# Eight and 32-row matmuls of a mixture-of-experts tail, issued over 128 rows with zeros behind

## The chip, the cores and the metric

The kernel runs on one core of a Trainium2 chip. The metric is the device time of one execution in microseconds. The engines are TensorE (PE, with its weight loads shown apart as PEld), VectorE (DVE), ScalarE (ACT), GpSimd (POOL) and SyncE (SP); transfers run on 16 DMA engines and are issued from SP or POOL.

## The reference

Three layers follow each other: a linear attention with random features, a dense layer with `h - tanh(h)`, and a mixture of eight experts. The change is in the third:

```python
def _moe2_ref(x, w_gate, w1, w2):
    N, D = x.shape                 # 2304, 512
    E = w_gate.shape[1]            # 8
    cap = N // E                   # 288
    flat = (x @ w_gate).flatten()
    order = np.argsort(-flat)
    assigned = -np.ones(N, dtype=np.int64)
    counts = np.zeros(E, dtype=np.int64)
    for idx in order:              # best score first
        tok, e = (int(idx) // E, int(idx) % E)
        if assigned[tok] >= 0 or counts[e] >= cap:
            continue
        assigned[tok] = e
        counts[e] += 1
    for e in range(E):
        mask = assigned == e
        h = np.maximum(x[mask] @ w1[e], 0.0)
        out[mask] = h @ w2[e]
```

So tokens go to experts by falling score, an expert is full at 288 tokens, and every expert computes two products over its 288 tokens.

## The kernel before

The kernel is one program whose order is set by a planner: every operation is entered with its engine, an assumed duration, the tiles it reads and writes and a due time (`plan.at`), and a list scheduler then writes the instructions of each engine in one fixed order. At run time each engine works through its list and waits on semaphores where a tile isn't ready.

The attention and the dense layer take the first 550 us or so. The dense layer's second product (L648, tiles `acc`) goes on beyond that for the last two of six blocks, until about 630 us. From about 545 us on the routing runs beside it, and from about 636 us the experts.

**Routing (`search_ops`, `route_ops`).** Experts are filled one after another; which one is next, and the score at which it is full, is searched digit by digit, seven digits for each of the first seven experts (the last takes what is left). For each digit DVE compares the scores with 15 to 31 thresholds (L1030), PE counts by nine products into 40 rows (L1036), DVE turns the counts into one number for each of the eight experts, in `d8` (8 rows, one column, L1057), and PE spreads these eight numbers over all 128 rows with one product over 8 rows (L1061: `d8` broadcast as the stationary operand, the 8x8 identity `id8` as the moving one). DVE reads the largest digit out of it (L1064) and makes the next thresholds. That is 7 x 7 = 49 products of 8 rows.

**Places (`place_ops`).** When an expert's tokens are known, 18 products (L1193) put the tokens' numbers in order; a copy (L1198) brings the result of 32 rows into `r1`, and one product over 32 rows (L1200) spreads it over 128. There are 8 of these.

**Gathers and experts (`expert_ops`).** For each expert POOL gathers its 288 rows of 512 numbers from DRAM in three pieces of 128, 128 and 32 rows (`xg`, L1289). PE transposes them: for each of four column groups c one PSUM tile takes three transposes, 128, 128 and 32 tokens wide (L1301 for experts 1 to 7, L1305 for expert 0). The 32-row piece is the third. ACT and DVE copy the 288 columns out as `xgH` and `xgL`. Then come the expert's products, each with 288 columns (L1333 to L1335 and L1352 to L1354), and at the end transposes back (L1364) and a scatter to DRAM. The routing of the following experts and the transposes of the next one are put between these products on PE's list, one small product at a time.

`pairs_ops` clears two tiles `pairs` on POOL (L1003) before the first search; DVE fills them (L993) and PE's counts read them.

The pieces come from a ring of three slots in the order of g, so the 32-row piece has had one slot of its own.

Of the kernel before, what the change touches and what calls it, by code (L numbers as in the profile page):

```python
# [8 lines left out]
F32 = mybir.dt.float32  # L9
F32R = mybir.dt.float32r  # L10
BF16 = mybir.dt.bfloat16
# [174 lines left out]
def tile_kernel(ctx, tc, q, k, v, omega, w_in, w_out, w_gate, w_gate_t, w1, w2, out, dbg=None):  # L186
    nc = tc.nc
# [4 lines left out]
    P = 128  # L192
# [701 lines left out]
    def r_setup():  # L894
# [10 lines left out]
        for i, wd in enumerate(WIDTH):  # L905
# [48 lines left out]
        nc.vector.memset(t["asg"], 0.0)  # L954
        t["mfull"] = c.tile([1, 1], BF16, name="mfull")
        nc.vector.memset(t["mfull"], -1.0e6)
        t["id8"] = c.tile([E, E], BF16, name="id8")
        nc.vector.tensor_copy(t["id8"], ident[:E, :E])
        rt.update(t)

    rings = {}


    SLOTS = {"wraw": (3, 4), "ewH": (0, 4), "ewL": (1, 11), "xg": (NG, NG), "xgH": (1, 2), "xgL": (1, 2),
             "hH": (0, 9), "hL": (0, 9), "yT": (0, 4)}

    def tmp(shape, dt, name, n=1):
        if name not in rings:
            rings[name] = plan.ring(shape, dt, name, [
                (wr[0], [f"r_{name}{i}" for i in range(SLOTS.get(name, (n, n))[0])], False)])  # L970
        return Buf(rings[name])
# [25 lines left out]
    pairs = []  # L997

    def pairs_ops():
        for i in range(2):  # L1000
            t = wr[0].tile([P, NTT, 32], BF16, name=f"pairs{i}")
            pairs.append(Buf(None, t))
            plan.op(POOL, 0.5, lambda e, t=t: nc.gpsimd.memset(t, 0.0), w=[pairs[i]])  # L1003
        first["i288"] = Buf(None, wr[0].tile([P, 1, CAP], I32, name="i288"))
        plan.op(POOL, 0.5, lambda e: nc.gpsimd.iota(first["i288"].t, pattern=[[1, CAP]], base=0, channel_multiplier=0),
                w=[first["i288"]])

    def search_ops(m, A2, rr8):
# [3 lines left out]
        for i, (tab, n, sh) in enumerate(rt["bits"]):  # L1012
# [33 lines left out]
            if 0 < i < len(WIDTH) - 1:  # L1046
# [3 lines left out]
                vec(0.2, lambda V, base=base, tab2=tab2, n2=n2, pre=pre: V.tensor_scalar(  # L1050
                    base.t[:, :n2], tab2, pre.t, flip.t, op0=OP.bitwise_or, op1=OP.bitwise_xor), r=[pre, flip], w=[base], after=cmps)

            cond, d8 = tmp([E, 32], F32, "cond"), tmp([E, 1], BF16, "d8")
            odd = tmp([E, 32], F32, "odd")
            vec(0.1, lambda V, odd=odd, cnt=cnt, n=n: V.tensor_scalar(
                odd.t[:, :n], cnt.t[32:32 + E, n:2 * n], -1.0, None, op0=OP.mult), r=[cnt], w=[odd])
            vec(0.16, lambda V, cond=cond, cnt=cnt, d8=d8, n=n, odd=odd: V.scalar_tensor_tensor(  # L1057
                cond.t[:, :n], cnt.t[:E, :n], rt["r8"], odd.t[:, :n], op0=OP.subtract, op1=OP.is_ge,
                accum_out=d8.t), r=[cnt, odd, rr8], w=[cond, d8])
            dig = Buf(rpr)  # L1060
            plan.op(PE, 0.05, lambda e, dig=dig, d8=d8: nc.tensor.matmul(  # L1061
                dig.t[:, :E], d8.t.to_broadcast([E, P]), rt["id8"], start=True, stop=True), r=[d8], w=[dig])
            d = tmp([P, 1], I32, "d", 3)
            vec(0.08, lambda V, d=d, dig=dig: V.tensor_reduce(d.t, dig.t[:, :E], axis=AX.X, op=OP.max), r=[dig], w=[d])  # L1064
            if i == 0:
# [104 lines left out]
    def place_ops(p, inc, acc):  # L1170
# [20 lines left out]
        def rows(e):  # L1191
            for j in range(NTT):
# [1 line left out]
                                 start=(j == 0), stop=(j == NTT - 1))  # L1194

        plan.op(PE, 0.55, rows, r=[lid, ohh], w=[pi])
        r1 = tmp([2 * LO, NHI], BF16, "r1")
        vec(0.08, lambda V: V.tensor_copy(r1.t, pi.t[:2 * LO, :NHI]), r=[pi], w=[r1])  # L1198

        plan.op(PE, 0.15, lambda e: nc.tensor.matmul(pr.t[:, :NHI], rt["spread"][:2 * LO], r1.t, start=True, stop=True),  # L1200
                r=[r1], w=[pr])
        rs = rt["rsel"]
        vec(0.08, lambda V: V.tensor_tensor(rs[:, :NHI], pr.t[:, :NHI], rt["hm"], op=OP.mult), r=[pr], w=[brsel])
# [77 lines left out]
    def expert_ops(p):  # L1281
# [2 lines left out]
        xg = []  # L1284
        plan.at = base + AT_GET if p else -98.0
        for g in range(NG):
            t = tmp([GS, DM], F32, "xg", NG)
            ix = idxs[p][g][1] if p else first["top"][g]
            plan.op(POOL, 1.03, lambda e, g=g, t=t, ix=ix: nc.gpsimd.indirect_dma_start(  # L1289
                out=t.t[:GN[g]], out_offset=None, in_=ms if p else ms[:(NTT - TPB) * P + 1, :],  # L1290
                in_offset=bass.IndirectOffsetOnAxis(ap=ix.t[:GN[g]].bitcast(U32), axis=0)),
                r=[ix], w=[t], after=stored if p else stored4, late=5.0)
            xg.append(t)
        plan.at = base + AT_TURN if p else -58.0
        for c in range(NC):
            tp = Buf(bank3)
            cs = slice(c * P, (c + 1) * P)

            def transposes(e, c=c, tp=tp):
                for g in range(NG):  # L1300
                    nc.tensor.transpose(tp.t[:, g * GS:g * GS + GN[g]], xg[g].t[:GN[g], c * P:(c + 1) * P], ident[:GN[g], :GN[g]])  # L1301

            def others(e, cs=cs, tp=tp):
                for g in range(NG):
                    nc.tensor.matmul(tp.t[:, g * GS:g * GS + GN[g]], xg[g].t[:GN[g], cs], ident[:GN[g], :GN[g]],  # L1305
                                     start=(g == 0), stop=False, is_transpose=True, skip_group_check=True)

            def lasts(e, cs=cs, tp=tp, t=0, i=0):
                nc.tensor.matmul(tp.t[:, :CAP], m5[t][i].t[:, cs], first["sel"].t[:, t, :], start=False,
                                 stop=(t == TPB - 1 and i == 1), skip_group_check=True)  # L1310

            if p:
                plan.op(PE, 0.38, transposes, r=xg, w=[tp])
            else:
                o = plan.op(PE, 0.38, others, r=xg, w=[tp])
                for t in range(TPB):
                    for i in range(2):
                        o = plan.op(PE, 0.12, lambda e, lasts=lasts, t=t, i=i: lasts(e, t=t, i=i),
                                    r=[m5[t][i], first["sel"]], w=[tp], after=[o])
            plan.op(ACT, 0.3, lambda e, c=c, tp=tp: copy(e, xH.t[:, c], tp.t[:, :CAP]), r=[tp], w=[xH])  # L1320
            plan.op(DVE, 0.37, lambda e, c=c, tp=tp: low(e, xL.t[:, c], tp.t[:, :CAP], xH.t[:, c]), r=[tp, xH], w=[xL])
# [274 lines left out]
```

## Time and profile before

| | |
|---|---|
| runs | 921.21 us median of 3 (918.92 to 921.49) |
| profiled execution | 916.65 us, its span 914.7 us |
| busy share of the span | PE 96%, PEld 84%, DVE 71%, ACT 51%, POOL 28% |
| granted TensorE clock, mean | 0.986 of full speed |
| transfers | 194.72 MB, mean 213 GB/s |

The page's slices show PE at 0.9 or more of nearly every slice, with one at 0.5 where the first search begins. Ends of matmuls in the trace are modelled and overlap the next start, so a matmul's price in a dense stream is read from the distance of two starts, and not from its duration.

### The profile page before, as it was taken

How to read it: one execution, taken by the hardware profiler on the slowest of the kernel's cores; microseconds unless marked ns; L12 is line 12 of the kernel's file. 1: busy time of each engine (PE TensorE's matmuls, PEld its weight loads, DVE VectorE, ACT ScalarE, POOL GpSimd, SP SyncE). 2: the span in 40 equal slices, each digit the busy share in tenths (PEclk: the TensorE clock that was granted, in tenths of full speed). 3: DMA queues.
4: the chain of work that ended last, by engine and by line, in shares of the span. 5: the costliest groups of instructions: out<-in, count | busy, mean ns of one | idle time of the engine just before them, and what ended most of it. 6: DMA issues, size and time to landing. Idle time of an engine off the chain costs nothing. (4 is left out here: it accounts for less than half of the span.)

```text
span 914.7 us, 17555 instructions
## 1 busy us (share of the span) xinstructions
PE 875.9 (96%) x6168; PEld 770.8 (84%) x6168; DVE 652.2 (71%) x1931; ACT 469.3 (51%) x1015; POOL 253.2 (28%) x271
## 2 busy tenths in 40 slices
PE   8988999999999999999999959899999999999995
PEld 6887888988989888989989937676889888999995
DVE  6899999866588779777778763527687786784520
ACT  5876554545457445655577640203366554465521
POOL 1223433333431345244313230000122322321211
PEclk9999999999999999999999999999999999999998
DMA  8988777876375666434677745845788886877600
GB/s 256 344 283 285 255 248 258 264 246 199 109 241 162 209 207 219 150 105 127 209 289 269 266 164 170 272 127 174 236 266 233 270 226 186 279 186 262 213 28 26
DMA packets 104365, 194.72 MB, mean 213 GB/s; under 512 B 28370, under 2 KB 42834, under 8 KB 104275
## 3 DMA queue, kind: packets, MB, share of 16 engines
q1 hardware_dynamic: 98610, 174.71, 58.0%
q0 software_dynamic: 5664, 18.88, 8.6%
q8 instruction: 49, 0.80, 0.4%
q14 instruction: 42, 0.34, 0.1%
HBM read 150.03 MB, written 34.08 MB: 201 GB/s over the span
## 5 line engine op out<-in xcount | busy, mean ns | idle before, releaser
L648 PE MATMUL acc<-wo,gL 128*128 128x512 f32 x288 | 114.9, 401 | 0.2 <-POOL gL L303 0.2
L601 PE MATMUL bk<-xH,wi 128*128 128x384 f32 x320 | 113.9, 356 | 0.9 <-DVE xt L500 0.9
L602 PE MATMUL bk<-xL,wi 128*128 128x384 f32 x320 | 107.8, 337 | 0.0
L603 PE MATMUL bk<-xH,iL 128*128 128x384 f32 x320 | 107.7, 337 | 0.0
L707 DVE SCALAR_TENSOR_TENSOR lw<-wf,raw 128x512 f32<-128x512 f32 x128 | 103.5, 808 | 2.9 <-POOL wf L704 1.4
L648 PE MATMUL acc<-wo,gH 128*128 128x512 f32 x240 | 101.1, 421 | 0.0
L303 POOL TENSOR_TENSOR gL<-s,gH 128x384 fp32r<-128x384 f32 x52 | 62.7, 1206 | 137.1 <-ACT gH L298 136.0
L648 PE MATMUL acc<-oL,gH 128*128 128x512 f32 x240 | 95.9, 400 | 0.3 <-DVE oL L303 0.3
L438 ACT ACTIVATE phi<-bk,nm 128x128 f32<-128x128 f32 x272 | 77.2, 384 | 34.4 <-DVE nm L441 34.1
L704 POOL TENSOR_TENSOR wf<-oL,wo 128x512 f32<-128x512 f32 x48 | 66.1, 1378 | 68.0 <-DMA oL<-low_wo 63.7
L298 ACT ACTIVATE gH<-s 128x384 fp32r<-128x384 f32 x80 | 42.2, 527 | 63.7 <-DVE s L628 46.3
L626 DVE SCALAR_TENSOR_TENSOR s<-s,bk 128x384 f32<-128x384 f32 x80 | 44.0, 550 | 41.7 <-ACT s L625 40.8
L648 PEld LDWEIGHTS acc<-wo,gL 128*128 128x128 f32 x288 | 54.9, 191 | 13.6 <-POOL gL L303 0.7
L601 PEld LDWEIGHTS bk<-xH,wi 128*128 128x128 f32 x320 | 60.7, 190 | 6.1 <-PE bk L480 1.1
L602 PEld LDWEIGHTS bk<-xL,wi 128*128 128x128 f32 x320 | 60.7, 190 | 2.7
L605 ACT ACTIVATE u<-bk 128x384 f32<-128x384 f32 x80 | 39.2, 491 | 45.2 <-PE bk L603 43.0
L603 PEld LDWEIGHTS bk<-xH,iL 128*128 128x128 f32 x320 | 60.4, 189 | 0.0
L628 DVE SCALAR_TENSOR_TENSOR s<-s,u 128x384 f32<-128x384 f32 x80 | 57.8, 722 | 1.1
L441 DVE TENSOR_REDUCE nm<-bk 128x4 f32<-128x512 f32 (+1 forms) x75 | 46.4, 631 | 12.7 <-PE bk L427 11.1
L648 PEld LDWEIGHTS acc<-wo,gH 128*128 128x128 f32 x240 | 45.7, 190 | 7.0
L648 PEld LDWEIGHTS acc<-oL,gH 128*128 128x128 f32 x240 | 46.0, 191 | 6.4 <-DVE oL L303 0.6
L625 ACT ACTIVATE s<-u,qbias 128x384 f32<-128x384 f32 x80 | 49.3, 616 | 3.8 <-DVE gL L303 1.4
(355 smaller groups left out, 2345.5 us busy)
## 6 DMA issues: line engine op xcount, KB each, us to landing
r_wraw<-in_moe_w_dram SPq DMA_DIRECT2D x48, 512.0 KB, 6.3
iL<-low_wi SPq DMA_DIRECT2D x80, 256.0 KB, 3.2
oL<-low_wo SPq DMA_DIRECT2D x80, 256.0 KB, 2.7
raw<-in_moe_w_in_dram SPq DMA_DIRECT2D x32, 512.0 KB, 5.1
raw<-in_moe_w_out_dram SPq DMA_DIRECT2D x32, 512.0 KB, 4.3
dw<-in_moe_w_dram SPq DMA_DIRECT2D x16, 512.0 KB, 5.9
w1l<-dw SPq DMA_DIRECT2D x16, 512.0 KB, 3.0
s_wraw<-in_moe_w_dram SPq DMA_DIRECT2D x16, 512.0 KB, 5.7
```

Source lines behind the costliest of these rows:

```text
L303: (nc.gpsimd if e == POOL else nc.vector).tensor_tensor(out, in_, high.bitcast(F32), op=OP.subtract)
L438: nc.scalar.activation(ph.t[:, i0 + i, :], pj.t[:, i * M:(i + 1) * M], AF.Exp, bias=nmx.t[:, i0 + i:i0 + i + 1])
L441: plan.op(DVE, 0.1 + 0.125 * n, lambda e, pj=pj, i0=i0, n=n: V.tensor_reduce(nmx.t[:, i0:i0 + n], pj.t[:, :n * M].rearrange("p (i m) -> p ...
L601: nc.tensor.matmul(ph(), piece(iH, c), xH.t[:, c, :], start=(c == 0), stop=False)
L602: nc.tensor.matmul(ph(), piece(iH, c), xL.t[:, c, :], start=False, stop=False)
L603: nc.tensor.matmul(ph(), piece(iL, c), xH.t[:, c, :], start=False, stop=(c == NC - 1))
L625: plan.op(ACT, 0.52, lambda e: nc.scalar.activation(s.t, ut(), AF.Square, bias=qbias), r=[u], w=[s], lag=2.8)
L626: plan.op(DVE, 0.52, lambda e: V.scalar_tensor_tensor(s.t, s.t, QD, ph(), op0=OP.add, op1=OP.mult), r=[p, s], w=[s], lag=3.4)
L628: plan.op(DVE, 0.65, lambda e: V.scalar_tensor_tensor(s.t, s.t, QC, ut(), op0=OP.mult, op1=OP.mult), r=[u, s], w=[s], lag=4.0)
L648: nc.tensor.matmul(acc[t].t, (gL if k == 2 else gH).t[:, c], (oL if k == 1 else oH).t, start=(f == 0 and k == 0), stop=(f == NF - 1 and k ...
L704: plan.op(POOL, 1.45, lambda e: nc.gpsimd.tensor_tensor(w.t, lo.t.bitcast(F32), wo[:, f, :].bitcast(F32), op=OP.add), r=[lo, wbuf["wo", f] ...
L707: x_reads.append(plan.op(DVE, 0.9, lambda e, i=i: nc.vector.scalar_tensor_tensor(scratch.t.bitcast(F32), w.t, 1.0, half(rows[i // 2], i % ...
```

## The change

Three kinds of small products are issued over 128 rows:

- `d8`, before a ring tile of 8 rows, is one lasting tile of 128 rows that is cleared once; DVE writes its first 8 rows as before. `id8` holds the first 8 columns of the 128x128 identity. L1061's product then has 128 rows.
- `r1` is one lasting tile of 128 rows, cleared once, of which the copy writes the first 32; L1200's product reads all 128 rows of it and of `spread`.
- The third piece of a gather is one lasting tile of 128 rows (`xg_rest`), cleared once on POOL in `pairs_ops`; the gather writes its first 32 rows. The three transposes of a column group all read 128 rows and write 128 columns of the PSUM tile; the copies still read 288 columns.

```diff
-        t["id8"] = c.tile([E, E], BF16, name="id8")
-        nc.vector.tensor_copy(t["id8"], ident[:E, :E])
+        t["id8"] = c.tile([P, E], BF16, name="id8")
+        nc.vector.tensor_copy(t["id8"], ident[:, :E])
+        for name, n in (("d8", 1), ("r1", NHI)):
+            t[name] = Buf(None, c.tile([P, n], BF16, name=name))
+            nc.vector.memset(t[name].t, 0.0)
...
-    SLOTS = {"wraw": (3, 4), "ewH": (0, 4), "ewL": (1, 11), "xg": (NG, NG), "xgH": (1, 2), "xgL": (1, 2),
+    SLOTS = {"wraw": (3, 4), "ewH": (0, 4), "ewL": (1, 11), "xg": (NG - 1, NG - 1), "xgH": (1, 2), "xgL": (1, 2),
...
     def pairs_ops():
+        first["xg"] = Buf(None, wr[0].tile([P, DM], F32, name="xg_rest"))
+        plan.op(POOL, 0.6, lambda e: nc.gpsimd.memset(first["xg"].t, 0.0), w=[first["xg"]])
...
-            cond, d8 = tmp([E, 32], F32, "cond"), tmp([E, 1], BF16, "d8")
+            cond, d8 = tmp([E, 32], F32, "cond"), rt["d8"]
...
-                accum_out=d8.t), r=[cnt, odd, rr8], w=[cond, d8])
+                accum_out=d8.t[:E]), r=[cnt, odd, rr8], w=[cond, d8])
...
-                dig.t[:, :E], d8.t.to_broadcast([E, P]), rt["id8"], start=True, stop=True), r=[d8], w=[dig])
+                dig.t[:, :E], d8.t.to_broadcast([P, P]), rt["id8"], start=True, stop=True), r=[d8], w=[dig])
...
-        plan.op(PE, 0.15, lambda e: nc.tensor.matmul(pr.t[:, :NHI], rt["spread"][:2 * LO], r1.t, start=True, stop=True),
+        plan.op(PE, 0.15, lambda e: nc.tensor.matmul(pr.t[:, :NHI], rt["spread"], r1.t, start=True, stop=True),
...
-            t = tmp([GS, DM], F32, "xg", NG)
+            t = tmp([GS, DM], F32, "xg", NG - 1) if g < NG - 1 else first["xg"]
...
-                    nc.tensor.transpose(tp.t[:, g * GS:g * GS + GN[g]], xg[g].t[:GN[g], c * P:(c + 1) * P], ident[:GN[g], :GN[g]])
+                    nc.tensor.matmul(tp.t[:, g * GS:(g + 1) * GS], xg[g].t[:, c * P:(c + 1) * P], ident,
+                                     start=True, stop=True, is_transpose=True)
```

The order of the instructions stays as it was on PE, ACT and SP. On POOL, at the place where the second half of the program begins, the list before is:

```order
L1003 MEMSET pairs_11785 128x576
L1003 MEMSET pairs_11786 128x576
L1005 IOTA i_11787 128x288
L1289 DMA r_xg_12390<-ms,r_ix_12290 128x512
L1289 DMA r_xg_12397<-ms,r_ix_12293 128x512
L1289 DMA r_xg_12410<-ms,r_ix_12295 32x512
```

and now:

```order
L1004 MEMSET xg_rest 128x512
L1008 MEMSET pairs_11790 128x576
L1008 MEMSET pairs_11791 128x576
L1010 IOTA i_11792 128x288
L1294 DMA r_xg_12386<-ms,r_ix_12288 128x512
L1294 DMA r_xg_12393<-ms,r_ix_12291 128x512
L1294 DMA xg_rest<-ms,r_ix_12293 32x512
```

One clearing stands ahead of the two of `pairs`; the third gather has a new target and the same place. On PE, in the transposes of one expert (tiles `bd` are PSUM banks), the list before is:

```order
L1301 MATMUL bd_16541<-ident,r_xg_16434 128x128
L1301 MATMUL bd_16541<-ident,r_xg_16446 128x128
L1301 MATMUL bd_16541<-ident,r_xg_16455 128x32
L1301 MATMUL bd_16547<-ident,r_xg_16434 128x128
L1301 MATMUL bd_16547<-ident,r_xg_16446 128x128
L1301 MATMUL bd_16547<-ident,r_xg_16455 128x32
```

and now:

```order
L1306 MATMUL bd_16484<-ident,r_xg_16378 128x128
L1306 MATMUL bd_16484<-ident,r_xg_16390 128x128
L1306 MATMUL bd_16484<-ident,xg_rest 128x128
L1306 MATMUL bd_16490<-ident,r_xg_16378 128x128
L1306 MATMUL bd_16490<-ident,r_xg_16390 128x128
L1306 MATMUL bd_16490<-ident,xg_rest 128x128
```

Nothing moved there; every third transpose writes 128 columns where it wrote 32.

## Rows read from the trace of the kernel before

**Rows 1.** Stretch, length; PE, PEld, DVE, ACT, POOL busy (instructions); clock, DMA share, GB/s.

```profile
554.00:583.00 29.00, 29.00 (x167) 20.79 (x167) 13.54 (x74) 1.52 (x3) 0.00 (x0) 1.00 0.60 184
...
636.00:690.00 54.00, 53.60 (x463) 47.37 (x460) 41.73 (x192) 28.19 (x44) 13.90 (x17) 1.00 0.84 245
```

**Rows 2.** PE's waits, 540 to 645, then 640 to 905: total us, times, longest.

```profile
PE rp L1036 <- DVE pairs L993: 6.4, 2, 4.4
PE rp L1061 <- DVE r_cond L1057: 1.5, 3, 0.6
...
PE be L1364 <- ACT s_yT L298: 0.2, 1, 0.2
```

**Rows 3.** Lines L1061 (with its waiter), L1200, L1301, L1305: ns min/median/max, starts, forms.

```profile
L1061 PE MATMUL rp<-id,r_d x49: 161/175/183, 548.3 to 810.9; 8*128 8x8 bf16 x49
...
  DVE r_d L1064: 37.8, 41
...
L1200 PE MATMUL rp<-r_r,spread x8: 178/178/179, 584.0 to 857.1; 32*128 32x18 bf16 x8
...
L1301 PE MATMUL bd<-ident,r_xg x45: 243/271/329, 664.2 to 867.2; 128*128 128x128 f32 x30, 32*128 32x32 f32 x15
...
L1301 PE MATMUL be<-ident,r_xg x39: 243/273/329, 664.7 to 868.8; 128*128 128x128 f32 x26, 32*128 32x32 f32 x13
...
L1305 PE MATMUL bd<-ident,r_xg x12: 243/272/328, 601.5 to 633.5; 128*128 128x128 f32 x8, 32*128 32x32 f32 x4
```

**Rows 4.** PE in order of time around one digit product: start us, us, what.

```profile
645.92 0.29 PE L1335 MATMUL be<-r_xgH,s_ewL 128*128 128x288 f32 x1
646.15 0.17 PE L1061 MATMUL rp<-id,r_d 8*128 8x8 bf16 x1
646.25 0.40 PE L1333 MATMUL be<-r_xgH,wi 128*128 128x288 f32 x1
646.49 0.30 PE L1334 MATMUL be<-r_xgL,wi 128*128 128x288 f32 x1
```

**Rows 5.** PE in order of time around the full-row pair L1125, L1126.

```profile
778.22 0.29 PE L1354 MATMUL bd<-s_hH,s_ewL 128*128 128x288 f32 x1
778.35 0.19 PE L1125 MATMUL rp<-r_M,onesb 128*128 128x36 bf16 x1
778.39 0.18 PE L1126 MATMUL rp<-r_M,tri 128*128 128x36 bf16 x1
778.42 0.38 PE L1352 MATMUL bd<-s_hH,wi 128*128 128x288 f32 x1
778.63 0.29 PE L1353 MATMUL bd<-s_hL,wi 128*128 128x288 f32 x1
```

**Rows 6.** PE in order of time, the twelve gather transposes of expert 6.

```profile
838.03 1.64 PE L1301 MATMUL bd<-ident,r_xg 128*128 128x128 f32 x9
839.60 0.61 PE L1301 MATMUL be<-ident,r_xg 128*128 128x128 f32 x3
840.14 0.40 PE L1352 MATMUL be<-s_hH,s_ewH 128*128 128x288 f32 x1
840.38 0.29 PE L1353 MATMUL be<-s_hL,s_ewH 128*128 128x288 f32 x1
```

**Rows 7.** PE in order of time, twelve transposes of results, all of 128 rows.

```profile
847.01 1.03 PE L1364 MATMUL bd<-ident,s_yT 128*128 128x128 f32 x8
847.88 0.60 PE L1364 MATMUL be<-ident,s_yT 128*32 128x128 f32 x4
848.24 0.38 PE L1333 MATMUL bd<-r_xgH,wi 128*128 128x288 f32 x1
848.45 0.30 PE L1334 MATMUL bd<-r_xgL,wi 128*128 128x288 f32 x1
```

**Rows 8.** POOL and DVE in order of time where the first search begins.

```profile
543.75 1.09 POOL L1003 MEMSET pairs<- 128x576 bf16 x2 [2.94 <-SPq L1459]
...
546.72 0.31 DVE L993 TENSOR_TENSOR pairs<-r_a,r_am 128x144 bf16<-128x144 f32 x1
```

More of the change, by code (lines that the diff above doesn't have):

```diff
@@ L1196, in place_ops @@
         plan.op(PE, 0.55, rows, r=[lid, ohh], w=[pi])
-        r1 = tmp([2 * LO, NHI], BF16, "r1")
-        vec(0.08, lambda V: V.tensor_copy(r1.t, pi.t[:2 * LO, :NHI]), r=[pi], w=[r1])
-        plan.op(PE, 0.15, lambda e: nc.tensor.matmul(pr.t[:, :NHI], rt["spread"][:2 * LO], r1.t, start=True, stop=True),
+        r1 = rt["r1"]
+        vec(0.08, lambda V: V.tensor_copy(r1.t[:2 * LO], pi.t[:2 * LO, :NHI]), r=[pi], w=[r1])
+        plan.op(PE, 0.15, lambda e: nc.tensor.matmul(pr.t[:, :NHI], rt["spread"], r1.t, start=True, stop=True),
                 r=[r1], w=[pr])
@@ L1300, in transposes @@
                 for g in range(NG):
-                    nc.tensor.transpose(tp.t[:, g * GS:g * GS + GN[g]], xg[g].t[:GN[g], c * P:(c + 1) * P], ident[:GN[g], :GN[g]])
+                    nc.tensor.matmul(tp.t[:, g * GS:(g + 1) * GS], xg[g].t[:, c * P:(c + 1) * P], ident,
+                                     start=True, stop=True, is_transpose=True)
             def others(e, cs=cs, tp=tp):
                 for g in range(NG):
-                    nc.tensor.matmul(tp.t[:, g * GS:g * GS + GN[g]], xg[g].t[:GN[g], cs], ident[:GN[g], :GN[g]],
+                    nc.tensor.matmul(tp.t[:, g * GS:(g + 1) * GS], xg[g].t[:, cs], ident,
                                      start=(g == 0), stop=False, is_transpose=True, skip_group_check=True)
```

## Prediction

> **What bounds the kernel now.** I read the table by stretch first. From 554 us to the end of the last expert TensorE (PE) has work in nearly every microsecond: 29.0 of 29.0 us while the last two blocks of the dense layer finish, 53.6 of 54.0 us in the first experts [rows 1]. A busy PE need not be a PE that gets on, so I read the waits next. From 640 to 905 us PE waits for another engine once, for 0.2 us; from 540 to 645 us the waits that matter are 6.4 us for VectorE's tile `pairs`, in two places where a search starts, and three short ones before the digit product L1061 [rows 2]. So from about 554 us on the time is what PE's own queue takes, in its fixed order, and every nanosecond between the starts of two neighbouring matmuls counts. The third view is therefore PE's instructions in order of time, read by the distances of their starts; busy times would hide what is looked for.
>
> There the small products show a cost that their size doesn't explain. In the stream of an expert's products the starts lie 0.13 us apart. Around one digit product (8 rows, 8 columns) they read 645.92, 646.15 for the product, 646.25 and 646.49: from the product before to the second one after, 0.57 us instead of 0.26, so one tiny product costs 0.31 us [rows 4]. A pair of equally small bf16 products that use all 128 rows (L1125 and L1126, 36 columns) reads 778.22, 778.35, 778.39, 778.42, 778.63: 0.41 us over the same stretch with two of them inside, and the first starts after the usual 0.13 us, not after 0.23 [rows 5]. The transposes say the same. Twelve of them with a 32-row piece in every third place take from 838.03 to 840.14, 2.11 us; twelve with 128 rows throughout take from 847.01 to 848.24, 1.23 us [rows 6, 7]. So the queue stops when it goes from 128 rows to fewer, and again on the way back.
>
> **The change part by part.** No instruction changes its place on PE, ACT, DVE or SP; the product of 8 or 32 rows is issued in the same place with 128. What is added is one clearing of the 128x512 piece on POOL, two small clearings and a wider copy of the 8x8 identity on DVE in the setup.
>
> *Digit products (L1061).* There are 49 [rows 3]. Three start a search and are waited for by PE anyway [rows 2]; these keep their wait, and gain at most what the way back costs, about 0.1 us, 0.3 us in all. Of the other 46, 39 stand alone in a stream of full products and 7 beside another small product. For one that stands alone the stretch goes from 0.57 us [rows 4] to that of one full-row product. The trace has that with two products inside, 0.41 us, and leaving out the 0.03 to 0.04 us of one gives 0.37 to 0.38 [rows 5]. The gain is thus 0.16 us at least (nothing saved for the one product fewer) and 0.20 at most; I take 0.19, which is 39 x 0.19 = 7.4 us. The 7 beside another product I count half, 0.7 us. Sum: 8.4 us.
>
> *The index product (L1200).* There are 8, each of 32 rows and 18 columns [rows 3]. Seven stand in the experts' stream at the price of a digit product: 7 x 0.19 = 1.3 us. The first is followed by a chain on DVE that PE waits for; I give it 0.1 us. Sum: 1.4 us.
>
> *The 32-row transposes (L1301, L1305).* There are 15 + 13 = 28 of them for experts 1 to 7 and 4 for expert 0 [rows 3], one behind each pair of full ones. Over twelve transposes and to the second product behind them the time is 840.38 - 838.03 = 2.35 us now, and 848.45 - 847.01 = 1.44 us where all have 128 rows [rows 6, 7]: 0.91 us for each of seven experts, 6.4 us. That already holds the price of moving 128 columns in place of 32. For expert 0 three of the four stand in the dense layer's stream, 3 x 0.23 = 0.7 us; the fourth falls where PE waits for DVE. Sum: 7.1 us.
>
> *What is added.* The piece is cleared on POOL ahead of the two clearings of `pairs`, 0.55 us each, which begin at 543.75 [rows 8]. Twice that price for it (four bytes an element in place of two) is the upper bound, 1.1 us; the first `pairs` would then be clear at 543.75 + 1.1 + 0.55 = 545.4, and DVE writes it at 546.72 [rows 8]. So it costs nothing, with 1.3 us to spare; without that cover it would lengthen the longest wait of PE by the same microsecond. Behind it on POOL are the second `pairs`, a table of numbers and, much later, the gathers. DVE's three setup steps lie in the dense layer's stage, where their price is some tenths of a microsecond beside PE's work; I set zero, at most 0.3 us. The gather into the 32-row piece used one buffer per expert before and does after, so no wait is added.
>
> *Sum.* 8.4 + 1.4 + 7.1 = 16.9 us. The profiled execution took 916.65 us, 914.7 of them its span, so it would take 899.8 us. It lies 4.6 us under the median of the runs, 921.21 us; from the median the sum gives 904.3 us.
>
> *What is late next.* DVE follows PE in the searches: after a digit product it waited 41 times for PE, 37.8 us together [rows 3], so an earlier product means an earlier answer, and the steps between an answer and the count that needs it don't shrink. Weight loads are the other feeder. Their engines were busy for 0.84 of the stretch from 636 to 690 us [rows 1], which is 45 us of work in 54; PE's part of the gain there is some 3 us.
>
> **The rivals.** *Part is given back.* The search's chain on DVE, or the loads with 0.84 of their engines' time used [rows 1], could take over in places, and PE would then wait for what it now finds ready. The experts' part of the gain is 5.8 + 1.3 + 6.4 = 13.5 us; with half of it turned into waits the time is 904.3 + 6.8 = 911.1 us. For it: experts 0 to 4 run with both feeders well used. Against it: not one wait above 0.2 us on PE in 265 us [rows 2], and in the last experts, which no search accompanies, there is nothing to take over.
>
> *The stall doesn't come from the rows, and the wider transposes cost extra.* The digit product reads a tile that DVE has only just written, and the full-row pair loads a constant; if it were that, or the change from one type to another, the stalls would stay, and the 32 transposes would move 128 columns in place of 32. A transpose of 128 columns takes 0.109 us of the queue (eight of them start from 847.01 to 847.88) [rows 7]; of 32 such, between nothing and all may be new, 0 to 3.5 us. I take all as the price of this case: 921.2 + 3.5 = 924.7 us, slower by 0.4%. It decides as soon as a 128-row product is preceded by the same 0.23 us. Against it: the transposes of rows 7 load a tile that ACT has just written and still follow at 0.109 us, and rows 5 show a change of type without a stop.
>
> *Rows don't matter and neither do columns.* Then nothing is saved and nothing is added, 921.2 us.
> The Trainium skill speaks for that: its page "TensorE: Matmul & The Clock Gate", section "LDWEIGHTS (loading the stationary operand)", says that a 32x128 weight load takes as long as a 128x128 one, since only columns count, and its table "Why this matters for your kernels" says that a single product with K=32 takes as long as one with K=128. By that padding is worth nothing. The durations here agree with it, the distances of the starts [rows 4, 5] don't, so I give it little.
>
> **How the numbers follow.** The full gain has 0.79, the part given back 0.15, no effect 0.03, the extra columns 0.03. The forecast is the first, 904.3 us. A gain of 0.20 us on each small product makes the sum 18.3 us at the upper end; with the lowest run of before, 918.92, that is 900.6 us, and from the profiled execution the sum gave 899.8. At the other end stands the part given back with 911.1. The range is 899.5 to 912 us. A measurement of this kernel can tell about 0.3%, 2.8 us, from no change; faster by more has 0.94, within it 0.03, slower by more 0.03.
>
> **What would show it.** In the changed kernel's trace the digit product should start 0.13 us behind its forerunner, and the second product behind it 0.37 to 0.41 us after the one ahead; twelve gather transposes should take 1.2 to 1.3 us where they took 2.11; PE should still wait for nothing worth naming from 640 us on. It would be wrong if the distance before the digit product stays at 0.23 us (then the rows aren't the cause), or if the distances shrink and PE shows new waits for DVE or for weights (then the gain moves into them). A wait for `pairs` that grows beyond 4.4 us would show that POOL's clearing isn't covered.

## The result

| | before | changed | ratio, 95% |
|---|---|---|---|
| first measurement, median (runs) | 920.07 us (6) | 908.92 us (6) | 0.9870, 0.9848 to 0.9892 |
| repeated | 919.15 us (13) | 906.84 us (4) | 0.9887, 0.9858 to 0.9917 |
| profiled execution, its span | 916.65, 914.7 us | 907.36, 905.5 us | |

The kernel became faster by 11.2 us, and by 12.3 us in the repetition. Forecast were 16.9 us and 904.3 us: the sign and the range held, and two thirds of the sum arrived, in the repetition nearly three quarters. The first time lies 4.6 us above the forecast and 2.2 us below 911.1 us, the price of the rival "part is given back"; the second lies nearer the forecast.

The distances between the starts of neighbouring matmuls are where the forecast made its bet. PE of the changed kernel in order of time around one digit product (start in us, modelled duration, line, operation, operands), to be held against [rows 4]:

```profile
642.57 0.30 PE L1341 MATMUL bd<-r_xgH,s_ewL 128*128 128x288 f32 x1
642.71 0.18 PE L1066 MATMUL rp<-id,d 128*128 128x8 bf16 x1
642.75 0.38 PE L1339 MATMUL bd<-r_xgH,wi 128*128 128x288 f32 x1
642.97 0.30 PE L1340 MATMUL bd<-r_xgL,wi 128*128 128x288 f32 x1
```

The product now starts 0.14 us behind its forerunner, where it was 0.23, and from the product before it to the second behind it are 0.40 us, where it was 0.57. This is the number to read; the duration in the second column even grew, from 0.17 to 0.18 us. PE at expert 6's twelve gather transposes, the first and the last of them, for [rows 6]:

```profile
830.74 0.38 PE L1306 MATMUL bd<-ident,r_xg 128*128 128x128 f32 x2
830.96 0.27 PE L1306 MATMUL bd<-ident,xg_rest 128*128 128x128 f32 x1
...
831.94 0.27 PE L1306 MATMUL be<-ident,xg_rest 128*128 128x128 f32 x1
831.97 0.38 PE L1358 MATMUL be<-s_hH,s_ewH 128*128 128x288 f32 x1
832.18 0.29 PE L1359 MATMUL be<-s_hL,s_ewH 128*128 128x288 f32 x1
```

Twelve transposes take from 830.74 to 831.97, 1.23 us in place of 2.11, and 1.44 us to the second product behind them in place of 2.35: the numbers of the full-row transposes in [rows 7], to 0.01 us.

PE's waits of the changed kernel, 545 to 640 us and then behind 640 us (total us, times, longest), for [rows 2]:

```profile
PE rp L1041 <- DVE pairs L996: 6.4, 2, 4.4
PE rp L1066 <- DVE r_cond L1062: 1.1, 2, 0.6
...
PE be L1370 <- ACT s_yT L298: 0.2, 1, 0.2
PE rp L1066 <- issue: 0.2, 1, 0.2
PE bd L1306 <- DMA xg_rest<-ms,r_ig: 0.2, 1, 0.2
PE rp L1066 <- DVE r_cond L1062: 0.2, 1, 0.2
PE bd L1306 <- DMA r_xg<-ms,r_ig: 0.2, 1, 0.2
```

The long wait for `pairs` is unchanged at 4.4 us, so the added clearing is covered. Behind 640 us one wait of 0.2 us became five: PE now meets DVE's answers and a gather. Both show in the order of time. First the transposes of expert 2, then a digit product, and the end of DVE's answer ahead of that digit product:

```profile
694.66 0.27 PE L1306 MATMUL bd<-ident,r_xg 128*128 128x128 f32 x1
695.11 0.33 PE L1306 MATMUL bd<-ident,r_xg 128*128 128x128 f32 x1 [0.18 <-DMA r_xg<-ms,r_ig]
695.64 0.33 PE L1306 MATMUL bd<-ident,xg_rest 128*128 128x128 f32 x1 [0.20 <-DMA xg_rest<-ms,r_ig]
...
688.18 0.29 PE L1341 MATMUL bd<-s_xgH,s_ewL 128*128 128x288 f32 x1
688.69 0.18 PE L1066 MATMUL rp<-id,d 128*128 128x8 bf16 x1 [0.22 <-issue]
...
688.56 0.07 DVE L1062 DVE_READ_ACCUMULATOR r_cond<-rp,rem,r_odd 8x1 bf16 x1
```

Expert 2's first transposes are 0.45 and 0.53 us apart where 0.11 would do: its gathered rows haven't landed. The digit product at 688.69 starts 0.51 us behind its forerunner, right behind DVE's answer, which ends at 688.56 + 0.07 = 688.63 ("issue" says only that the profile shows no one who released PE). The wait list counts only the idle part of such a gap; the distance shows all of it.

POOL's and DVE's rows where the first search begins, for [rows 8]:

```profile
545.26 0.52 POOL L1004 MEMSET xg_rest<- 128x512 f32 x1 [3.05 <-SPq L1465]
545.72 1.10 POOL L1008 MEMSET pairs<- 128x576 bf16 x2
...
548.15 0.31 DVE L996 TENSOR_TENSOR pairs<-r_a,r_am 128x144 bf16<-128x144 f32 x1
```

The piece took 0.52 us, and both `pairs` were clear at 546.82, 1.3 us before DVE wrote the first. (All of this stands 1.4 us later than before since this execution had lost that much earlier, where the program is the same.)

### The profile page after: what moved, and what is told of

Same layout as the page of the kernel before. It is cut to its first block, busy times and chain, and to the rows that moved or that the text cites. A ratio compares the mean times of both kernels' runs of the same rounds, so it can differ in the third digit from the quotient of the medians.

```text
span 905.5 us, 17561 instructions
## 1 busy us (share of the span) xinstructions
PE 866.9 (96%) x6168; PEld 770.9 (85%) x6168; DVE 651.0 (72%) x1933; ACT 467.1 (52%) x1015; POOL 251.9 (28%) x272
## 5 line engine op out<-in xcount | busy, mean ns | idle before, releaser
L707 DVE SCALAR_TENSOR_TENSOR lw<-wf,raw 128x512 f32<-128x512 f32 x128 | 105.4, 824 | 2.9 <-POOL wf L704 1.4
L628 DVE SCALAR_TENSOR_TENSOR s<-s,u 128x384 f32<-128x384 f32 x80 | 52.8, 660 | 1.1
```

Source lines behind the costliest of these rows:

```text
L628: plan.op(DVE, 0.65, lambda e: V.scalar_tensor_tensor(s.t, s.t, QC, ut(), op0=OP.mult, op1=OP.mult), r=[u, s], w=[s], lag=4.0)
L707: x_reads.append(plan.op(DVE, 0.9, lambda e, i=i: nc.vector.scalar_tensor_tensor(scratch.t.bitcast(F32), w.t, 1.0, half(rows[i // 2], i % ...
```

## The experiments

"Distances" are differences between the starts of PE's 6,168 products. From 544 us on each is compared with the same one in the first trace of the kernel before, unless another is named, and the differences are summed by kind. A small product's stretch runs from the product before it to the second one behind it.

**The digit products alone (e1).** On the kernel before:

```diff
-        t["id8"] = c.tile([E, E], BF16, name="id8")
-        nc.vector.tensor_copy(t["id8"], ident[:E, :E])
+        t["id8"] = c.tile([P, E], BF16, name="id8")
+        nc.vector.tensor_copy(t["id8"], ident[:, :E])
+        t["d8"] = Buf(None, c.tile([P, 1], BF16, name="d8"))
+        nc.vector.memset(t["d8"].t, 0.0)
...
-                dig.t[:, :E], d8.t.to_broadcast([E, P]), rt["id8"], start=True, stop=True), r=[d8], w=[dig])
+                dig.t[:, :E], d8.t.to_broadcast([P, P]), rt["id8"], start=True, stop=True), r=[d8], w=[dig])
```

> The change's digit products alone: d8 and id8 have 128 rows, the index product and the gathers' transposes stay as before. Theory (PE's queue stops on the way from 128 rows to fewer and back; what is lost of the gain is lost where PE overtakes what feeds it): the distances around a digit product fall from 0.57 to 0.39 us as in the whole change, 7.6 us in the trace of the whole change by my count of distances from 544 us on, and little is lost since PE overtakes less: 6 to 7.5 us faster than before, about 913.5 us. Rival (the lost part is chance, half-speed stretches of the clock that have nothing to do with how far PE gets ahead): a share of the measured 11.2 us as of the counted 15.4, 5.5 us, about 914.5 us. Rival (part of it came from elsewhere, such as tiles that lie at other addresses): distances as in the whole change, but a time that doesn't follow them.

916.69 us (10 runs) against 920.20 (25 runs), ratio 0.9962 (0.9941 to 0.9984): 3.5 us, some 3 us less than I had put. The interval, 1.5 to 5.4 us, leaves out the theory's 6 to 7.5 and just misses the rival's 5.5. The stretches of the digits shrank by 6.1 us in its trace, 0.18 at the median of those that stand alone, so the products did their part. (Counted like this the first trace of the whole change has 6.8, not the 7.6 of my expectation.) PE waited for DVE's `r_cond` 0.9 us behind 640 us, and products that ran at the lower clock in this trace (granted 0.50 from 588 to 595 and from 636 to 639 us) lost 2.1 us. The timed runs had a mean granted clock of 0.979, those of before 0.981; over the 25 runs of before the time falls by 0.46 us for each 0.001 of clock, so about 1 us of the miss goes with that.

**The transposes alone (e2).** On the kernel before, the other half:

```diff
+        first["xg"] = Buf(None, wr[0].tile([P, DM], F32, name="xg_rest"))
+        plan.op(POOL, 0.6, lambda e: nc.gpsimd.memset(first["xg"].t, 0.0), w=[first["xg"]])
...
-                    nc.tensor.transpose(tp.t[:, g * GS:g * GS + GN[g]], xg[g].t[:GN[g], c * P:(c + 1) * P], ident[:GN[g], :GN[g]])
+                    nc.tensor.matmul(tp.t[:, g * GS:(g + 1) * GS], xg[g].t[:, c * P:(c + 1) * P], ident,
+                                     start=True, stop=True, is_transpose=True)
```

> The change's transposes alone: the 32-row piece has 128 rows and the transposes 128 columns, the digit and index products stay at 8 and 32 rows. Theory: twelve transposes take 1.2 us in place of 2.1, 6.4 us counted, less what waits for gathers: 5 to 6.4 us faster, about 914.5 us; with the digits alone the two gains add up to more than the 11.2 us of both with the index product's 1.4 taken off. Rival (no shared limit): 4.5 us, and the two add up to 9.8 us.

915.78 us (10 runs), ratio 0.9941 (0.9917 to 0.9964): 4.4 us at the medians, 5.4 by the ratio. With e1's 3.5 and the index product's 1.4 that makes 9.3 or 10.3 us, against 11.2 or 12.0 for all of the change, each with about 2 us of uncertainty. Within that the parts add up, as the rival had it and not the theory: nothing here shows a shared limit that lets either part alone have the whole, or a part that only pays beside the other.

**Eight rows, but 128 columns to move (e3).** On the kernel before:

```diff
-        t["id8"] = c.tile([E, E], BF16, name="id8")
-        nc.vector.tensor_copy(t["id8"], ident[:E, :E])
+        t["id8"] = c.tile([E, P], BF16, name="id8")
+        nc.vector.tensor_copy(t["id8"], ident[:E, :])
...
-                dig.t[:, :E], d8.t.to_broadcast([E, P]), rt["id8"], start=True, stop=True), r=[d8], w=[dig])
+                dig.t[:, :P], d8.t.to_broadcast([E, P]), rt["id8"], start=True, stop=True), r=[d8], w=[dig])
```

> The kernel before, with the digit product made longer in place of taller: 8 rows still, but 128 columns where it had 8 (the identity's first 8 rows, all columns; the answer still reads 8). Theory (rows): the product still starts 0.23 us behind its forerunner, and the next but one 0.24 us behind the next; the 120 columns more add up to 0.05 us each: 0 to 2.5 us slower than before. Rival (the stop belongs to very short products, whatever their rows): the stop goes, 0.57 us falls to about 0.4, and the kernel is 6 to 8 us faster.

923.95 us (10 runs), ratio 1.0032 (1.0001 to 1.0063): slower, by 3.8 us at the medians and 2.9 by the ratio, a little more than the 0 to 2.5 that I had put. PE around one of its digit products:

```profile
648.14 0.29 PE L1335 MATMUL bd<-r_xgH,s_ewL 128*128 128x288 f32 x1
648.36 0.23 PE L1061 MATMUL rp<-id,r_d 8*128 8x128 bf16 x1
648.52 0.41 PE L1333 MATMUL bd<-r_xgH,wi 128*128 128x288 f32 x1
648.76 0.29 PE L1334 MATMUL bd<-r_xgL,wi 128*128 128x288 f32 x1
```

The stops before and behind stay (0.22 and 0.24 us), and the product itself takes 0.16 us of the queue in place of 0.10. So the stop doesn't come from a product being short: with 128 columns to move and 8 rows it stops just the same; with 8 columns to move and 128 rows (642.71 us above) it doesn't. The stretch is 0.62 us where it was 0.57; 49 x 0.05 = 2.5 us is most of the loss.

**The counting products with 128 columns to load (e5).** On the changed kernel. The counts (L1041) already used 128 rows, but loaded 40 columns:

```diff
-                        nc.tensor.matmul(cnt.t[:32 + E, :2 * n].rearrange("p (a n) -> p a n", a=2),
-                                         A2.t[:, j:j + 2].rearrange("p a e -> p (a e)")[:, :32 + E],
+                        nc.tensor.matmul(cnt.t[:, :2 * n].rearrange("p (a n) -> p a n", a=2),
+                                         A2.t[:, j:j + 4].rearrange("p a e -> p (a e)"),
```

> The changed kernel, with the counts' products made as wide as the array: nine products of a digit load 128 columns of pairs where they loaded 40, so the result has 128 rows, of which the same are read. No instruction moves. Theory, widened (a stop comes with fewer than 128 columns of the stationary operand too): the first of a group starts 0.13 us behind its forerunner in place of 0.22, and the way back shortens from 0.11 and 0.24 to 0.03 and 0.22; with 54 groups that is some 10 us in distances, of which the search's chain on DVE takes a part back: 5 to 8 us under the changed kernel, 901 to 904 us. Rival (only rows matter): distances and time as in the changed kernel, 909 us. Rival (DVE is already the limit of the searches): distances fall and PE waits for DVE instead, 907 to 909 us.

901.48 us (4 runs), ratio to before 0.9790 (0.9757 to 0.9823): 7.4 us under the changed kernel's first measurement. PE around one block of five counts, in the changed kernel and then in this one:

```profile
640.51 0.29 PE L1341 MATMUL be<-r_xgH,s_ewL 128*128 128x288 f32 x1
640.74 0.32 PE L1041 MATMUL rp<-r_cmp,pairs 128*40 128x62 bf16 x5
640.99 0.40 PE L1339 MATMUL be<-r_xgH,wi 128*128 128x288 f32 x1
641.23 0.29 PE L1340 MATMUL be<-r_xgL,wi 128*128 128x288 f32 x1
```

```profile
640.63 0.29 PE L1341 MATMUL be<-r_xgH,s_ewL 128*128 128x288 f32 x1
640.77 0.32 PE L1041 MATMUL rp<-r_cmp,pairs 128*128 128x62 bf16 x5
640.93 0.38 PE L1339 MATMUL be<-r_xgH,wi 128*128 128x288 f32 x1
641.15 0.29 PE L1340 MATMUL be<-r_xgL,wi 128*128 128x288 f32 x1
```

From the product before to the second behind: 0.72 us, then 0.52 us, the same 0.2 us as at a digit product. So missing columns of the loaded operand stop the queue as missing rows do, and "only the rows" falls. Against the first trace of the changed kernel the stretches of its 54 blocks of counts shrank by 8.8 us, 0.20 at the median; PE's waits for DVE behind 640 us grew to 2.5 us.

**The rest of the small products too (e6).** On e5, the ordering products (18 in a row) and the pair that settles an expert:

```diff
-                nc.tensor.matmul(pi.t[:2 * LO, :NHI], lid.t[:, j].rearrange("p a l -> p (a l)"), ohh.t[:, j],
+                nc.tensor.matmul(pi.t[:, :NHI], lid.t[:, j:j + 4].rearrange("p j a l -> p (j a l)"), ohh.t[:, j],
...
-                nc.tensor.matmul(rp.t[:E, :1], gs.t, rt["ones"][:, :1], start=True, stop=False)
-                nc.tensor.matmul(rp.t[:E, :1], oh.t[0:1, :], rt["mfull"], start=False, stop=True)
+                nc.tensor.matmul(rp.t[:, :1], gs.t, rt["ones"][:, :1], start=True, stop=False)
+                nc.tensor.matmul(rp.t[:, :1], oh.t, rt["mfull"], start=False, stop=True)
```

> The kernel with the wide counts, and also the last two small products made 128 rows and 128 columns: the 18 products that put an expert's tokens in order load 128 columns where they loaded 32, and the pair that settles the remaining places (8 columns, and one row) loads 128x128 each, with zeros. In the list a few instructions near the end change places with their neighbours. Theory (every operand short of 128 in either direction stops the queue): 8 groups and 7 pairs shed 0.18 to 0.25 us each, 3.2 us in distances; with the part that DVE takes, 899 to 900.5 us against 901.5. Rival (DVE is the limit by now): 901.5 us, with longer waits of PE for DVE.

900.56 us (4 runs), ratio 0.9785 (0.9766 to 0.9804) to 920.64 for before: the fastest kernel of the study, 20.1 us under before, though what it adds to e5 is within the uncertainty. Its waits for DVE behind 640 us, and then one row of 18 ordering products with the product that follows, in the first trace of before and in e6:

```profile
PE rp L1072 <- DVE r_odd L1066: 1.8, 2, 0.9
PE rp L1072 <- DVE r_cond L1068: 1.6, 3, 0.6
```

```profile
718.95 0.61 PE L1193 MATMUL rp<-r_ohh,r_lid 128*32 128x18 bf16 x18
719.50 0.40 PE L1333 MATMUL bd<-r_xgH,wi 128*128 128x288 f32 x1
...
712.17 0.61 PE L1204 MATMUL rp<-r_ohh,lid 128*128 128x18 bf16 x18
712.64 0.38 PE L1345 MATMUL bd<-r_xgH,wi 128*128 128x288 f32 x1
```

PE waits 3.4 us for DVE now, 0.9 more than in e5. The row itself gains: it takes 0.47 us to the next product in place of 0.55, and its whole stretch, from the product before (718.73 and 712.04 us) to the second behind (719.74 and 712.86), 0.82 in place of 1.01. Against e5 seven of the eight rows gain 0.17 to 0.19 us each. The eighth, at 642.39 us, gains nothing, since the count behind it waits for DVE's `r_cmp`, which is ready at 642.99. So a row of eighteen pays for one stop, as a single product does.

**A second trace of each kernel (e9, e12).** No edit.

> The kernel before once more, for a second profile of it. The first profiled execution, 916.65 us, lies below every timed run (917.17 to 924.59), so distances counted against it may put down as lost what the kernel before loses as well in most executions. If so, this one shows about 1 us of PE's waits for digits and one or two half-speed stretches of the clock more than the first, at about 920 us. If not, it repeats the first, and the losses counted against it stand.

> The changed kernel once more, unchanged, for a second trace and more times beside the others on the same chip: 908.9 within 1 us. If the half-speed stretch at 635 us and the waits at the digits are the change's doing, this trace has them too; if they are the luck of one execution, it has them elsewhere or not at all.

920.42 us for before (one run), and 906.84 us (4 runs) for the changed kernel. PE's waits behind 640 us, e9 first, then e12:

```profile
PE rp L1061 <- DVE r_cond L1057: 1.0, 2, 0.6
PE rp L1036 <- DVE r_cmp L1030: 0.6, 1, 0.6
PE be L1364 <- ACT s_yT L298: 0.2, 1, 0.2
```

```profile
PE bd L1306 <- DMA r_xg<-ms,r_ig: 0.2, 1, 0.2
PE be L1370 <- ACT s_yT L298: 0.2, 1, 0.2
```

The kernel before waits for DVE's answers too, 1.6 us in this execution, and between 530 and 600 us it stays 6.8 us longer at the lower clock; the profile that the forecast rests on was one without. And the changed kernel has an execution with next to none. So the waits at the digits in the first trace of after don't come with the change as such, as far as two traces of each can tell. The clock differs by execution too. Stretches (PE, PEld, DVE, ACT and POOL busy, granted clock, DMA share, GB/s) of the first and the second trace of the changed kernel:

```profile
634.60:638.00 3.40, 3.40 (x15) 3.25 (x16) 3.34 (x13) 2.00 (x2) 0.69 (x1) 0.50 1.05 302
```

```profile
632.50:638.00 5.50, 4.21 (x36) 3.68 (x35) 5.44 (x23) 2.42 (x3) 1.76 (x2) 1.00 1.04 327
```

At 634.6 us the first trace runs 3.4 us at 0.50, the lower level of 1.2 GHz, just behind a row of short waits, and places its products 0.24 us apart in place of 0.13; that lost some 1.1 us. The second trace is at full clock there. What recurs in both, and in e11 below, is expert 2's late gather (the stretch of its twelve transposes takes 0.2, 0.2 and 0.6 us more than before, where 0.91 less were due) and a count at 633 us that waits 0.3 us longer.

**DVE's subtractions left out (e7, e8).** On before and on the changed kernel, the low halves of the weights that DVE makes are not made:

```diff
-                for k in range(2):
-                    h = slice(k * FX // 2, (k + 1) * FX // 2)
...
-                    plan.op(DVE, 0.62, lambda e, h=h, H=H, L=L, raw=raw: low(e, L.t[:, h], raw.t[:, h], H.t[:, h]),
-                            r=[raw, H], w=[L])
+                L = H
...
```

> The kernel before with VectorE relieved: it leaves out the low halves of the expert weights that VectorE computes (60 operations of 0.68 us, 41 us of its time beside the experts); the products that read them read the high halves again, so PE does the same work on other numbers. Half of a pair, to be read against the changed kernel with the same left out. If PE is the limit of the kernel before (my reading), the time stays near before's, 917 to 920 us; if VectorE held it back already, 914 us or less.

> The changed kernel with VectorE relieved in the same way (the low halves of the expert weights that VectorE computes are left out, the products read the high halves again). Theory (the part of the gain that is missing, 11.2 of a counted 15 to 16 us, went to waits for VectorE): against its partner without the change it gains 14 to 16 us. Rival (it went elsewhere: the clock's half-speed stretches, the stage that waits for VectorE's first answers, or was never there): 10 to 12 us.

928.74 us (ratio 1.0087, 1.0060 to 1.0115) and 912.91 us (0.9923, 0.9907 to 0.9940). The pair differs by 15.8 us, as the theory had it, but I don't count it: each is slower than its full sister, by 8 and by 4 us, though an engine has less to do. The planner, given fewer steps, had set another order, the same for both: at 1,444 of PE's 6,168 places the product writes another tile than in the full kernels. PE's row at the transposes of one of the last experts in e7, and the stretch that follows:

```profile
819.71 1.15 PE L1297 MATMUL bd<-ident,r_xg 32*128 32x32 f32 x4 [1.86 <-DMA r_xg<-ms,r_ig]
...
819.80:826.60 6.80, 6.80 (x27) 5.55 (x28) 1.83 (x4) 1.64 (x4) 0.00 (x0) 0.50 0.60 161
```

PE idles 1.86 us for the gather, and from then on 6.8 us go by at the lower clock, as 6.8 us do from 638.9 us on; e8's trace has no such stretch behind 640 us. So the 15.8 us hold what the clock did in e7 and stand for another order, and can't be set against the 11.2 us of the full kernels.

**The same with the order kept (e10, e11).** The subtractions stay in their places, on 64 columns:

```diff
-
-                    plan.op(DVE, 0.62, lambda e, h=h, H=H, L=L, raw=raw: low(e, L.t[:, h], raw.t[:, h], H.t[:, h]),
+                    L.short = True
+                    plan.op(DVE, 0.62, lambda e, h=slice(k * FX // 2, k * FX // 2 + 64), H=H, L=L, raw=raw: low(e, L.t[:, h], raw.t[:, h], H.t[:, h]),
...
-                    nc.tensor.matmul(q, L.t[:, fs], xH.t[:, c], start=False, stop=(c == NC - 1))
+                    nc.tensor.matmul(q, (H if L.short else L).t[:, fs], xH.t[:, c], start=False, stop=(c == NC - 1))
...
```

> The kernel before with every instruction in its place, but each of DVE's two subtractions for an expert's weight chunk that is split on the core works on 64 columns instead of 512, and the product that would read the low half reads the high half again: this part of the result is left out. DVE's queue is lighter by some 90 subtractions of 0.5 us each, PE's queue has the same rows. Theory (the digit and counting products that wait for DVE do so because its queue holds these subtractions): the kernel before waits 0 to 1.6 us for DVE's answers behind 640 us in its two profiles, so 918.5 to 920.5. Rival (the waits have nothing to do with this queue): 920.5 within 1 us, the same waits in the trace.

> The changed kernel with the same shortening (the same part of the result is left out), again with every instruction in its place. Theory: what the changed kernel gives back to DVE's answers (about 1.0 us at the digits and 0.5 to 1 at the counts behind 640 us) goes away: 906.0 to 907.5, a pair difference to the same shortening of before of 12 to 13.5 us, and no distance over 0.25 us at a digit product behind 646 us. Rival (what is given back is the clock's half-speed stretch and the wait for a gather, and DVE's answers only fill time that PE would have lost anyway): 908.4 to 909.5, a pair difference of 11 within 1.

918.44 us (10 runs) against 919.15 for before, ratio 0.9993 (0.9969 to 1.0017); 905.90 us (4 runs), 0.9879 (0.9829 to 0.9929), beside 906.84 us for the changed kernel on the same chip. PE's waits behind 640 us in e11:

```profile
PE bd L1306 <- DMA r_xg<-ms,r_ig: 0.8, 1, 0.8
PE be L1370 <- ACT s_yT L298: 0.2, 1, 0.2
```

Not one wait for DVE is left behind 640 us, in either trace, and around every digit product in the experts' stream of e11 the stretch of three distances is at most 0.40 us, where the first trace of the changed kernel has seven of 0.50 to 0.77. (The shortened subtractions are 60, at 0.22 us each where they took 0.68, and not some 90.) The time moved by 0.7 us in the one and 0.9 in the other, both within their uncertainty, and the pair differs by 12.5 us where the full kernels differ by 12.3. So nothing here shows that the missing third of the forecast went into DVE's queue: at the digits its waits cost 1.1 us in the first trace of the changed kernel and 0.3 in the second. The two windows don't decide it. The numbers lie by the theory's (905.90 is a tenth under 906.0, and 12.5 lies in 12 to 13.5), but both windows were priced from 908.9, and beside 906.84 the shortening gave 0.9 us. The four runs of e11 have an interval of 5 us to either side, so the times alone leave room for more.

## Why the prediction was right, and what it sized wrongly

- **The bound and the mechanism.** Right: PE's queue sets the end, what counts in it is the distance of starts, and it stops where a product uses fewer rows than its neighbour. e1 and e2 show it apart for the digits and the transposes; e3 and e5 show that it is the rows and columns in use, not the product's length. The Trainium skill, page "TensorEngine Tiling (Array Packing)", section "Tiling Modes", says that a change of tiling mode drains TensorE. The traces fit that with 0.2 us a visit, for 8 rows as for 40 columns; that a drain is what happens in these 0.2 us no run shows. The list of modes in the same section of the Trainium skill goes down to 32 rows, by which an 8-row product right behind a 32-row one needs no second drain. The trace of before agrees, it has such a pair 0.04 us apart:

```profile
794.19 0.18 PE L1200 MATMUL rp<-r_r,spread 32*128 32x18 bf16 x1
794.23 0.16 PE L1061 MATMUL rp<-id,r_d 8*128 8x8 bf16 x1
```

- **The digits: 8.4 us forecast, 7.6 counted in the second trace of after.** Forty stand alone in a stream, and the median gain of one is 0.178 us in that trace as in the first; I had taken 0.19. That is 7.1 us; the other nine, beside another small product or at a search's start, gained 0.8 us together, where I had put 1.0 for ten. DVE's late answers took back 0.3 us in the second trace and 1.1 us in the first. (The sum of 18.3 us at the upper end has 0.20 us for all 49 digit products, but not for the index products.)
- **The index products: 1.4 forecast, 1.4 counted.**
- **The transposes: 7.1 us forecast, 5.5 counted.** In the second trace the stretches of experts 3 to 7 gained 0.78 to 0.91 us each, of expert 1 0.71, of expert 0 0.95 where I had put 0.7; 0.3 of this belongs to four digit products that stand in or beside them. Expert 2 lost 0.18 us in place of gaining 0.91. The last piece of its gather on POOL and its first transpose on PE, in the first trace of before and in the second of after:

```profile
689.75 0.88 POOL L1289 DMA_INDIRECT r_xg<-ms,r_ig  x1 [0.30 <-DVE r_base L1050]
697.42 0.56 PE L1301 MATMUL bd<-ident,r_xg 128*128 128x128 f32 x3
...
685.96 0.88 POOL L1294 DMA_INDIRECT xg_rest<-ms,r_ig  x1 [0.30 <-DVE r_base L1055]
692.85 0.27 PE L1306 MATMUL bd<-ident,r_xg 128*128 128x128 f32 x1
```

From issue to landing the piece takes 7.4 us in the one and 7.8 in the other, so it landed at 697.11 and at 693.78 us: 3.3 us sooner, while PE came to its transposes 4.6 us sooner. That is the place where "part is given back" came true, through a transfer that I hadn't listed; I had written that no wait is added since the buffer is the same, and it was not the buffer that PE waited for.
- **What is late next: set to nothing.** This is the term that was wrong. The products themselves gave 7.6 + 1.4 + 5.5 = 14.5 us of the 16.9 forecast, so 2.4 us were terms sized too large, 1.1 of them at expert 2's gather. From 544 us on the second trace of after is 12.0 us shorter than the first of before. The other 2.5 us are 0.3 at the count at 633 us, 0.6 spread thinly over 1,300 products of the experts, 0.3 in smaller pieces, and 1.3 in the counts and dense-layer products behind the two waits for `pairs`, where this execution stays at the lower clock for longer (mean granted clock from 587 to 597 us 0.66, against 0.83). Whether that is the change's doing isn't shown: the first trace of after has 0.83 there too, those of e1 and e11 have 0.66. The two traces of after against the two of before give 10.6, 12.0, 13.6 and 15.0 us, 12.8 on average, and the timed 11.2 and 12.3 lie among them. Of the signs that I had named for it, a new wait for DVE showed with 0.4 us in PE's list for the first trace (with the 0.2 us put down to "issue") and not at all in the second; a wait for weights showed in neither.
- **The rivals.** "Part is given back" was priced at half of the experts' gain, 6.8 us; some 2 to 3 us were, through the gather above all and DVE's answers in part. The first time lies nearer to this rival's number than to mine, in part because terms were sized too large, and the range held since it took in the rival: the forecast of 904.3 us itself was missed by 4.6 us, more than the 2.8 us that I had named as what a measurement can tell. The wider transposes cost nothing extra (830.74 to 831.97 us), and the stop before a digit product that stands alone was gone.
- **What is added: nothing, right.** The clearing on POOL took 0.52 us where I had allowed 1.1, and the second trace of after reaches the end of the part that is the same in both kernels at 542.35 us, the first of before at 542.49, so the setup cost nothing that shows.
- **The base.** The profiled execution of before, 916.65 us, was quicker than any of the 45 runs that were timed beside the experiments (917.17 to 924.59 us). Moving the sum to the median was right, though the median of six runs came to 920.07 where that of three had been 921.21. Reading "not one wait above 0.2 us" from that one execution as what the kernel always does was not right.

## What to carry to other kernels

A small product amid full ones costs more than its own time: look at the starts of its neighbours, not at its duration, and if they open by 0.1 us on each side, pad it to the neighbours' rows and columns with zeros that are written once. Count a row of small ones as one visit: eighteen in a row gained 0.19 us together, as much as one that stood alone. And before a sum of small gains is believed to the last microsecond, look in a second execution at what stands next to ready.

## What the runs showed beyond that

- Fewer columns of the loaded operand stop the queue as fewer rows do (0.72 to 0.52 us over a block of counts), which made e5 and e6 7 to 8 us faster than the changed kernel's first measurement. It is not so everywhere: transposes that load 32 columns follow full ones without a stop [rows 7], and what sets them apart no run here shows.
- Leaving work out of a planned kernel made it 8 us slower, with another order; what of the 8 us each change of place costs isn't shown. A load is better taken away inside the instruction, with the order kept.
- From 540 us on the granted clock drops to 0.50 for stretches of 3.4 to 10 us, mostly behind a place where PE waited, and for how long differs by execution: over 25 runs of before the mean clock went from 0.975 to 0.988, and the time fell by 0.46 us per 0.001 of it.
